# Sliding-window attention beside an MLP: output scaled while turned, rows of two heads dealt into spare rows, and a fixed order of instructions

## The chip, the core and the metric

The kernel runs on one core of a Trainium2 chip. The metric is the device time in microseconds, the median of three runs. A core has a matrix engine (TensorE, PE in the profile, with its weight loads as PEld), VectorE (DVE), ScalarE (ACT), GpSimd (POOL), SyncE (SP), which here only issues transfers, and 16 DMA engines. Matrix products go to PSUM, eight banks of 128 partitions by 512 f32; everything else lives in SBUF.

## The reference

One token sequence of 2048 with 448 features is normalized. Branch A is a local attention (16 heads of 28 features, each query sees eight keys at distances 0, 2, ..., 14) with an output projection. Branch B is an MLP of width 1792. The result is x + A * silu(B).

```python
x = A_x
xn = _layernorm(x, axis=-1)
# A: 16 heads of 28, window 8, dilation 2
qkv = (xn @ wqkv).reshape(B, S, 3, H, Dh)
idx = pos[:, None] - 2 * jnp.arange(8)[None, :]      # masked where < 0
logits = jnp.einsum("bhsd,bhswd->bhsw", q, kg) * Dh ** -0.5
o = jnp.einsum("bhsw,bhswd->bhsd", softmax(logits), vg)
s = o.reshape(B, S, D) @ wo
# B
h = gelu(xn @ w1 + b1)
g = silu(h @ w2 + b2)
return x + s * g
```

## The kernel before

**Tiles and stages.** Tokens are held with the even ones first and the odd ones behind, so that a window with dilation 2 becomes one of eight neighbours. There are 16 tiles of 128 tokens and four chunks of four tiles. For each tile, DVE takes statistics and normalizes (`stats`, `norm`), the normalized rows are turned (by TensorE for the first four tiles, by transposing DMAs on SP's queue for the others), and q, k and v are projected (L595, L618). q and k are turned by transposing DMAs; v goes out to memory and comes back in the layout of the windows. FF1 (L671) makes the hidden layer of a chunk in 14 blocks, with gelu on ACT (L675); FF2 (L703, L725) brings it back, and `gate` computes silu: on DVE the bias (L737), on ACT tanh or silu (L749, L744), on DVE the product (L753).

**Row halves.** 448 = 3 x 128 + 64. To use the array fully, most products run as 64-row passes, two tiles at a time: `pair` (L534) issues the passes of tile a on the upper 64 rows beside those of tile b on the lower 64, then the other way round, each tile into its own bank. Between the two halves the banks change their row half, so an empty instruction on POOL's queue (L551) waits for the first half, and the second half waits for it. TensorE does other passes in between. For q, k, v and FF1 a pair has 4 + 3 passes a tile, since the last 64 features stand on both halves of the rows; for FF2 it has 14 + 14.

**Attention.** Nine visits of 228 tokens each (224 in the middle). A visit has the scores (L770, four banks), exp on ACT (L779), masks on DVE (L785) and the values (L799), which leave two banks: bank a holds, on partitions 32g to 32g+27, a head's 28 output features, on partition 32g+28 the sum of the weights, in columns the tokens of two heads per group. `output_of` divides, per bank, by four instructions on DVE: a 32x32 transpose of the bank to `dt` (L808), the reciprocal of the sums (L812), a second transpose that spreads the reciprocals over the partitions (L817), and the product of bank and spread reciprocals into `oT` (L822). The bank is free only after the last of them.

**Output projection.** `oT` and `wo` have four kt of 128 rows; in each group of 32 rows, 28 are features and four are not (of wo they are zero, set by POOL at the start, L370). `final` (L853) makes the output projection. Tiles 0 to 13 go in pairs, with all four kt in either half:

```python
pair(job(t), job(t + 1), prio, False, (range(KT),), (range(KT),))
```

Tiles 14 and 15 have four passes of the full 128 rows each (L871), between which the last parts of their FF2 run. `gated` (L877) multiplies by the gate (L885, L883), adds x (L890) and sends the tile out on SP's queue (L894).

**Order.** Every instruction or group of them is a task of `_Plan`, with an engine, a cost, its dependencies, buffers that it takes and gives back, and a priority. `run` (L102) is a list scheduler: of the tasks of an engine that could start first, it takes the one with the highest priority (PRIO, LATER, NUDGE). The emitted program has one fixed order for each engine, so a wait of one instruction holds all behind it on that engine. At the start, tasks of TensorE that multiply constants (L346) fill its time until the plan's 8 us; those that would start later are left out.

Of the kernel before, what the change touches and what calls it, by code (L numbers as in the profile page):

```python
# [14 lines left out]
SLACK = 0.12  # L15
TABLE = 1.28
SWITCH = 0.095
TILED = 30
BURST = 3.5
NUDGE = {  # L20
    61: 4, 64: -20, 140: -165, 160: -221, 163: -244, 165: -29, 397: 111, 413: -37, 490: 163, 669: -149,
}
LAST = 352
SAME = 20
# [24 lines left out]
class _Task:  # L49
    __slots__ = ("eng", "cost", "deps", "fn", "prio", "take", "give", "slots",  # L50
# [3 lines left out]
class _Plan:  # L54
# [7 lines left out]
    def add(self, eng, cost, fn, deps=(), prio=0, take=(), give=(), tail=0.0, table=(), limit=None,  # L62
            mode=128):
# [4 lines left out]
        t.fn, t.prio, t.give, t.tail, t.table, t.limit = fn, prio, give, tail, table, limit  # L68
# [9 lines left out]
        t.prio += NUDGE.get(t.seq, 0)  # L78
# [6 lines left out]
    def _at(self, t, e, free):  # L85
        at = free.get(e, 0.0)
        for p, n in t.take.items():
            if len(p.free) < n or p.fifo and p.fifo[0] is not t:
                return None
            at = max(at, sorted(p.free)[n - 1][0] + HOP)  # L90
        if t.table and self.table not in t.table:
            at += TABLE
        for d in t.deps:
            at = max(at, d.end - d.tail if d.on == e else d.end + HOP)
        if e == "PE" and t.mode != self.mode:
            at = max(at, free.get(e, 0.0) + SWITCH)
        return at

    def _ready(self, t):
        return max([d.end - d.tail if d.on == "DMA" else d.end + HOP for d in t.deps], default=0.0)  # L100

    def run(self):  # L102
# [4 lines left out]
        free = {}  # L107
        self.table = None
        self.mode = 128
        ready = [t for t in self.tasks if not t.ndep]  # L110
        order = []
        while ready:
            cand = []
            for t in ready:
                ways = []
                for e, c in zip(t.eng, t.cost):
                    at = self._at(t, e, free)
                    if at is not None:
                        ways.append((at + (c if len(t.eng) > 1 else 0.0), at, e, c))
                if ways:  # L120
                    _, at, e, c = min(ways)
                    cand.append((at, t, e, c))
            if not cand:
                raise RuntimeError("the plan is stuck: " + str([(t.seq, t.eng, t.fn.__qualname__) for t in ready[:20]]))
            first = min(cand, key=lambda k: k[0])
            near = [k for k in cand if k[2] == first[2] and k[0] <= first[0] + SLACK]
            tiled = first[2] == "PE" and self.mode < 64
            at, t, e, c = min(near, key=lambda k: (self._ready(k[1]) if k[2] == "DMA" else -k[1].prio - (TILED if tiled and k[1].mode < 64 else SAME if k[2] == "PE" and k[1].mode == self.mode else 0),
                                                   k[0], k[1].seq))
            if t.limit is not None and at > t.limit:  # L130
                t.fn, c = None, 0.0
            t.on, t.start = e, at
            if e == "PE" and t.fn is not None:
                self.mode = t.out or t.mode
            if t.table and self.table not in t.table:
                self.table = t.table[0]
            free[e] = at + c
            t.end = at + c + t.tail
            for p, n in t.take.items():
                got = sorted(p.free)[:n]  # L140
                for g in got:
                    p.free.remove(g)
                t.slots[p] = [g[1] for g in got]
                t.after += [g[2] for g in got]
                if p.fifo is not None:
                    p.fifo.pop(0)
            for p, owner, i in t.give:
                p.free.append((t.end, owner.slots[p][i], t.seq))
            ready.remove(t)
            order.append(t)  # L150
            for u in t.users:
                u.ndep -= 1
                if not u.ndep:
                    ready.append(u)
        assert len(order) == len(self.tasks)
        self.order = sorted(order, key=lambda t: (t.start, t.seq))
        self.span = max(t.end for t in order)
        return self

# [19 lines left out]
def kernel(  # L179
# [62 lines left out]
    b1r = sb("b1r", [P, P])  # L242
# [6 lines left out]
    oT = sb("oT", [P, KT, S])  # L249
# [7 lines left out]
    zero = sb("zero", [P, H * 32])  # L257
# [4 lines left out]
    def ring(name, n, shape, dt=BF16, fifo=False):  # L262
# [5 lines left out]
    p_dt = ring("dt", 2, [P, 512], F32)  # L268
    p_rd = ring("rd", 2, [P, H], F32)
    p_y = ring("y", 2, [P, D], F32)  # L270
    p_t = ring("t", 2, [P, D], F32)
# [6 lines left out]
    p_h = ring("h", 28, [P, CH], fifo=True)  # L278
    p_v = ring("v", 3, [P, 4, H // 2, 32], fifo=True)
# [6 lines left out]

    PRIO = {
        "project": (54, 6.5, -1, -796,),
        "project2": (-47, -24.5, -697.5, -972,),
        "values": (-60, -238.5, -708, -812.5,),  # L290
        "attn": (332.5, 150, 124.5, 209.5, 61, 182.5, 339.5, 196.5, 276,),
        "ff1": (75, 107.5, 161, -24.5, -31, 92, 171.5, -1, -8, 117.5, 54, 79.5, 64, 6.5, 40, 96.5,
            13.5, 22.5, -0.5, 30, 190, 161.5, 181, 165.5, 181, 129, 104, 64.5,),
        "gelu": (-8, 79.5, 28, 194.5,),
        "ff2": (91.5, -34.5, -96.5, 114.5, 129.5, 89, -831.5, 135, 120, 180.5, 59, 104, 147.5, 131,
            -12.5, -48,),
        "final": (207.5, 2, 71.5, -16.5, 55.5, -2, 174.5, 203, 37, 65.5, -16, 162.5, 87.5, 134, 36,
            -5,),
        "norm": (131, 11, 219.5, 294, 62, 220, -31, 168.5, 7, 29.5, 162.5, 183.5, -110, 4.5, 164,
            134,),  # L300
        "loads": (227.5, 186, 183, 40, 129.5, 100, 27, -66,),
        "stats": (49, 32, 205.5, 205.5, 112, 82, 130.5, -5, 44.5, 27, 147.5, 207.5, 114, 203.5,
            217, 161,),
        "turn_x": (198, 4.5, 200, 12.5, 259, 121, 98.5, 186.5, 57, 57, 72, 135.5, 79, 58, 135, 88,),
        "turn_qk": (18.5, 126, 116, 140, -16, 32.5, 118.5, -91.5, 79.5, 15, 161.5, 121.5, 77.5,
            162.5, 166, -17.5,),
        "move_v": (129.5, 145.5, 200.5, 147.5, 126, 210.5, 218.5, 150, 100.5,),
        "store_v": (103, 80.5, 21.5, 52, 191, 92, 149, 31, 118, 150, 333.5, -0.5, 106, 223.5, 214,
            111,),
        "spread": (-10.5, 75.5, 298, 99.5, 52.5, 186.5, 149.5, -55, 104,),  # L310
        "copies": (187, 4, 219, 15.5, 90, 177, 88.5, 31, 29, 20.5, 182, 51, 204.5, 49.5, 24,),
    }
    LATER = {"swap": 191.5, "qk": 27, "v": 148, "gelu": 32.5, "exp": 149.5, "mask": -4394.5, "pv": -29.5, "recip": 100, "os": 224, "y": 202, "tanh": 79.5, "g": 204, "sg": 165.5, "o": 222.5}
# [28 lines left out]
    t_on = plan.add("DMA", 0.7, lambda _: None, (), 100)  # L342
    t_warm = t_on
    for i in range(48):
        def fn(k, n=512 if i < 9 else P):
            nc.tensor.matmul(buf(p_b, k)[:, :n], ones[:, :P], ones[:, :n], start=True, stop=True)  # L346
        t_warm = plan.add("PE", 0.427 if i < 9 else 0.107, fn, [t_warm], 1000 if i < 12 else -1000, take=(p_b,), limit=8.0)
        t_warm.give = ((p_b, t_warm, 0),)
    t_eps = plan.add("DVE", 0.07, memset("vector", eps_t[:], EPS), [t_on], prio=99)
    t_eps = plan.add("DVE", 0.07, memset("vector", half_t[:], -0.5), [t_eps], prio=99)  # L350
# [5 lines left out]
    t_ident = plan.add("POOL", 0.55, mk_ident, [t_on], prio=99)  # L356

    t_qz = [plan.add("DVE", 0.08, memset("vector", q[:, :, :, DH:], 0.0), [t_on], prio=95) for q in qk_tok]
    t_vw = [plan.add("DVE", 0.08, memset("vector", v[:, :, :, DH:], 1.0), [t_on], prio=96) for v in v_tok]
    t_kz = plan.add("DVE", 0.12, memset("vector", qkT[:, :, :, :PAD], 0.0), [t_on], prio=92)  # L360
# [330 lines left out]
    def ff2(t, prio):  # L691
        c, j = divmod(t, TPC)
        if t >= NT - 2:
            t_g[t] = []
            for cs, n, end in parts(t)[:1]:
                ff2_part(t, cs, n, end, prio - 0.1 * end)
# [359 lines left out]
```

## Time and profile before

| | us |
|---|---|
| runs | 152.48, 152.04, 152.18 |
| median | 152.18 |
| span of the profiled execution, first to last instruction | 150.4 |

The span leaves out what lies around it in a run, 1.78 us against the median; the time of the profiled execution as a whole is not given beside its span. In the profile, a line of a group reads: source line, engine, operation, output <- input, partitions x elements and type, count | busy us, mean ns of one | idle time of the engine just before it, and what ended it. Lines of the chain and of the timeline begin with start and length in us. DMA shares in the page are means over 16 engines.

### The profile page before, as it was taken

How to read it: one execution, taken by the hardware profiler on the slowest of the kernel's cores; microseconds unless marked ns; L12 is line 12 of the kernel's file. 1: busy time of each engine (PE TensorE's matmuls, PEld its weight loads, DVE VectorE, ACT ScalarE, POOL GpSimd, SP SyncE). 2: the span in 40 equal slices, each digit the busy share in tenths (PEclk: the TensorE clock that was granted, in tenths of full speed). 3: DMA queues.
4: the chain of work that ended last, by engine and by line, in shares of the span. 5: the costliest groups of instructions: out<-in, count | busy, mean ns of one | idle time of the engine just before them, and what ended most of it. 6: DMA issues, size and time to landing. Idle time of an engine off the chain costs nothing.

```text
span 150.4 us, 5216 instructions
## 1 busy us (share of the span) xinstructions
PE 146.1 (97%) x2173; PEld 76.9 (51%) x2173; DVE 113.7 (76%) x276; ACT 96.0 (64%) x168; POOL 18.4 (12%) x51
## 2 busy tenths in 40 slices
PE   7999999999999999999999999999999999999990
PEld 2644444544455555558556554445556445555460
DVE  3876850495546889899997989497998978995962
ACT  3365877658496594785788648888567497822020
POOL 7425530201750000011000000000000000000000
PEclk9999999999999999999999999999999999999999
DMA  4999869889999957159967994521120000001212
GB/s 155 327 314 362 126 124 159 261 119 361 185 161 197 72 100 139 37 114 226 125 201 175 147 256 128 125 74 38 36 65 7 0 0 4 4 0 61 63 63 63
DMA packets 38470, 19.47 MB, mean 129 GB/s; under 512 B 24887, under 2 KB 37758, under 8 KB 38446
## 3 DMA queue, kind: packets, MB, share of 16 engines
q1 hardware_dynamic: 37790, 17.84, 53.9%
q0 software_dynamic: 512, 1.18, 4.5%
q8 instruction: 17, 0.28, 0.8%
q10 hardware_dynamic: 144, 0.11, 0.2%
q14 instruction: 7, 0.06, 0.1%
HBM read 9.42 MB, written 3.94 MB: 89 GB/s over the span
## 4 chain that ended last, share of the span: by engine, by line
PE 97%; DVE 0%; ACT 0%; issue 0%
PE bank L671 28%; PE bank L703 25%; PE bank L595 14%; PE bank L618 7%; PE bank L863 7%; PE bank L799 4%; PE bank L725 4%; PE bank L346 3%; PE bank L770 3%; PE bank L871 1%; PE bank L519 1%; DVE sg L883 0%; ACT w_in L744 0%; PE bank L503 0%; DVE o L890 0%; PE bank L723 0%
## 5 line engine op out<-in xcount | busy, mean ns | idle before, releaser
L671 PE MATMUL bank<-xnT,w 64*128 64x512 bf16 x392 | 44.1, 376 | 0.0
L675 ACT ACTIVATE h<-bank,b 128x512 bf16<-128x512 f32 x56 | 34.5, 687 | 11.7 <-PE bank L671 11.5
L703 PE MATMUL bank<-w,h 64*128 64x448 bf16 x392 | 40.2, 349 | 0.0
L671 PEld LDWEIGHTS <-w 64*128 64x128 bf16 x392 | 18.8, 94 | 22.1
L703 PEld LDWEIGHTS <-h 64*128 64x128 bf16 x392 | 18.6, 94 | 16.8
L595 PE MATMUL bank<-w_in,xnT 64*128 64x448 bf16 (+1 forms) x212 | 24.8, 350 | 0.0
L779 ACT ACTIVATE E<-bank 128x456 bf16<-128x456 f32 (+1 forms) x36 | 16.9, 554 | 9.9 <-PE bank L770 8.6
L331 ACT CAST qk_tok<-bank 128x448 bf16<-128x448 f32 x25 | 12.3, 539 | 5.9 <-PE bank L595 4.8
L595 PEld LDWEIGHTS <-xnT 64*128 64x128 bf16 (+1 forms) x212 | 10.8, 94 | 9.4 <-DVE xnT L333 0.2
L808 DVE STREAM_TRANSPOSE dt<-bank 128x480 f32<-128x480 f32 (+1 forms) x18 | 12.1, 673 | 4.5 <-PE bank L799 4.5
L618 PE MATMUL bank<-w_in,xnT 64*128 64x448 bf16 (+1 forms) x106 | 14.0, 350 | 0.0
L863 PE MATMUL bank<-wo,oT 64*128 64x448 bf16 x112 | 12.6, 349 | 0.0
L817 DVE STREAM_TRANSPOSE dt<-rd 128x480 f32<-128x480 f32 (+1 forms) x18 | 12.1, 675 | 0.6
L822 DVE TENSOR_TENSOR oT<-bank,dt 128x456 bf16<-128x456 f32 (+1 forms) x18 | 11.4, 632 | 0.6
L785 DVE TENSOR_TENSOR E<-E,m_gen 128x456 bf16<-128x456 bf16 (+1 forms) x32 | 10.8, 390 | 0.0
L443 DVE BATCH_NORM_STATS2 st<-x_sb 128x6 f32<-128x448 bf16 x16 | 9.5, 606 | 1.7 <-DMA x_sb<-in_A_x_dram 1.7
L333 DVE CAST qk_tok<-bank 128x448 bf16<-128x448 f32 x7 | 4.3, 620 | 8.6 <-PE bank L595 8.6
L737 DVE TENSOR_TENSOR y<-bank,b 128x448 f32<-128x448 f32 x15 | 8.7, 619 | 1.9 <-PE bank L703 1.8
L749 ACT ACTIVATE t<-y 128x448 f32<-128x448 f32 x12 | 6.7, 583 | 4.0 <-DVE y L737 4.0
L484 DVE TENSOR_SCALAR xn<-x_sb,mv,rstd 128x448 bf16<-128x448 bf16 x16 | 6.3, 393 | 3.6 <-POOL rstd L466 3.4
L744 ACT ACTIVATE w_in<-y 128x448 bf16<-128x448 f32 x3 | 1.7, 577 | 10.9 <-DVE y L737 10.9
L863 PEld LDWEIGHTS <-oT 64*128 64x128 bf16 x112 | 5.8, 94 | 4.8 <-issue 0.2
(76 smaller groups left out, 143.5 us busy)
## 6 DMA issues: line engine op xcount, KB each, us to landing
v<-v_hbm SPq DMA_DIRECT2D x16, 128.0 KB, 3.2
out_dram<-o SPq DMA_DIRECT2D x15, 112.0 KB, 2.0
v_hbm<-v_tok SPq DMA_DIRECT2D x13, 128.0 KB, 3.5
w<-in_B_w_dram SPq DMA_DIRECT2D x2, 672.0 KB, 6.7
w_in<-in_A_wqkv_dram SPq DMA_DIRECT2D x3, 336.0 KB, 4.2
x_sb<-in_A_x_dram SPq DMA_DIRECT2D x4, 224.0 KB, 4.1
w<-in_B_w_dram SPq DMA_DIRECT2D x2, 448.0 KB, 7.8
w<-in_B_w_dram SPq DMA_DIRECT2D x2, 336.0 KB, 8.9
```

Source lines behind the costliest of these rows:

```text
L331: nc.scalar.copy(o, i)
L595: return nc.tensor.matmul(ps[:, :D], xnT[r, kt, cs], w, start=start, stop=stop)
L618: return nc.tensor.matmul(ps[:, :D], xnT[r, kt, k0:k0 + P], w, start=start, stop=stop)
L671: return nc.tensor.matmul(ps[:], w1[r, kt, ms], xnT[r, kt, cs], start=start, stop=stop)
L675: nc.scalar.activation(buf(p_h, own, i)[:], buf(p_b, own, i)[:], ACT.Gelu_apprx_tanh, bias=b1[:, mt:mt + 1])
L703: return nc.tensor.matmul(ps[:, :D], buf(*h_at[(c, mt)])[r, cs], w2[r, mt, :], start=start, stop=stop)
L779: nc.scalar.activation(buf(p_E, k)[:, :8 * n], buf(p_b, a, at + i)[:, :8 * n], ACT.Exp, scale=SCALE)
L785: nc.vector.tensor_tensor(out=E, in0=E, in1=m[:, :, :, :n].rearrange("p i g q -> p (i g) q"), op=ALU.mult)
L808: nc.vector.transpose(buf(p_dt, k)[:, :32 * m], buf(p_b, po, i)[:, :32 * m])
L817: nc.vector.transpose(buf(p_dt, d)[:, :32 * m].rearrange("p (b c) -> p b c", c=32), buf(p_rd, r)[:, :m].unsqueeze(2).to_broadcast((P, m, 32)))
L822: nc.vector.tensor_tensor(out=oT[:, a::2, q:q + 4 * n1], in0=buf(p_b, po, i)[:, :n].rearrange("p (l q) -> p l q", l=2), in1=buf(p_dt, d)[: ...
L863: return nc.tensor.matmul(ps[:, :D], oT[r, kt, t * P:(t + 1) * P], wo[r, kt, :], start=start, stop=stop)
```

## The change

It has three parts.

1. **Attention output.** Per bank: a transpose of all 512 columns to an f32 tile (the bank is free after it), the reciprocal, the product in the turned layout (tokens on partitions, 28 features of a head together), written as bf16 over the same tile, and a bf16 transpose into `oT`. Before this last transpose four small copies per visit, on POOL or ACT, put the rows of the two heads that bank 1's second half holds on partitions 0 to 63 into the four spare columns of every group of 32. So kt 0, 1 and 2 have 128 feature rows each and kt 3 has 64, on its lower half.
2. **Output projection.** wo is loaded in the same arrangement (eight loads instead of four, no zeroing), and its 64 rows of kt 3 are copied to the upper half. `final` runs three kt in the first half of a pair and four in the second. For odd tiles up to 13 the lower rows of kt 3 of `oT` are copied to the upper ones; for tiles 14 and 15 the upper rows are set to zero.
3. **Order.** The scheduler and its priorities go; a list ORDER names the tasks by number, in the order in which they are placed; a negative number takes the second engine of a task that has two. Buffers change too: `dt`, `y` and `t` share one ring of six, `b1r` and `zero` use buffers of other rings. Three output tiles (8, 9, 10) leave in two transfers each.

```diff
-NUDGE = {
...
+ORDER = [
+    53, 49, 50, 126, 1, 82, 64, 54, 56, 52, 2, 3, 4, 5, 83, 6, 7, 8, 9, 10, 11, 86, 87, 88, 66, 90, 68, 70, 72, 74,
...
+]
+TWICE = (8, 9, 10)
...
-        while ready:
...
+        for n in ORDER:
+            self._place(self.tasks[max(n, ~n)], int(n < 0))
...
-    oT = sb("oT", [P, KT, S])
+    oT = sb("oT", [P, KT, S + 32])
...
-    p_dt = ring("dt", 2, [P, 512], F32)
+    b1r = p_E.bufs[1][:, :P]
+    p_dt = p_y = p_t = ring("wide", 6, [P, 512], F32)
...
-    t_wo = [plan.add("POOL", 1.6, memset("gpsimd", wo[:], 0.0), [t_ident], prio=98)]
...
-                            c0, c1 = (4 * h + s) * n, (G * (s % 2) + g) * n
+                            c0, c1 = 256 * h + s * n, (G * (s % 2) + g) * n
...
+    def turned_in(d):
+        return buf(p_dt, d)[:].bitcast(BF16)[:, :512].rearrange("p (l b c) -> p l b c", l=2, c=32)
+
+    def output_of(b, po):
         q, n1 = VIS[b]
+        d, m = [], []
+        for a in range(2):
+            def f5(k, a=a):
+                nc.vector.transpose(buf(p_dt, k)[:], buf(p_b, po, a)[:])
+            d.append(plan.add("DVE", dve(512), f5, [po], take=(p_dt,), give=((p_b, po, a),)))
+        for a in (1, 0):
+            def f6(k, a=a):
+                nc.vector.reciprocal(buf(p_rd, k)[:], buf(p_dt, d[a])[:].rearrange("p (b c) -> p b c", c=32)[:, :, DH])
+            r = plan.add("DVE", 0.25, f6, [d[a]], take=(p_rd,))
+
+            def f7(k, a=a, r=r):
+                nc.vector.tensor_tensor(out=turned_in(d[a]).rearrange("p l b c -> p (l b) c")[:, :, :DH],
+                                        in0=buf(p_dt, d[a])[:].rearrange("p (b c) -> p b c", c=32)[:, :, :DH],
+                                        in1=buf(p_rd, r)[:].unsqueeze(2).to_broadcast((P, H, DH)), op=ALU.mult)
+            m.insert(0, plan.add("DVE", dve(D), f7, [r], give=((p_rd, r, 0),)))
+        for a in range(2):
+            moved = []
+            for x in range(2):
+                def f8(k, a=a, x=x):
+                    i = turned_in(d[1])[:64, 1, :, :DH].rearrange("p b (g c) -> p g b c", c=4)[:, 3 * x + a:3 * x + a + 3:2]
+                    o = turned_in(d[a])[64 * x:64 * x + 64, :, :, DH:]
+                    if k.on == "ACT":
+                        nc.scalar.copy(o, i)
+                    else:
+                        nc.gpsimd.tensor_copy(o, i)
+                moved.append(plan.add(("POOL", "ACT"), (0.3, 0.21), f8, [m[0], m[1]]))
+
+            def f9(_, a=a):
+                nc.vector.transpose(oT[:, a::2, q:q + 256], turned_in(d[a]).rearrange("p l b c -> p l (b c)"))
+            o = plan.add("DVE", dve(512), f9, moved + turned_out[a][-1:], give=((p_dt, d[a], 0),))
...
+                    t_up[t] = [plan.add(("POOL", "ACT"), (0.35, 0.26), f, t_oT[t])]
+                elif t >= NT - 2:
+                    t_up[t] = [plan.add("POOL", 0.25, memset("gpsimd", oT[:64, 3, t * P:(t + 1) * P], 0.0), t_oT[t])]
...
-            pair(job(t), job(t + 1), prio, False, (range(KT),), (range(KT),))
+            pair(job(t), job(t + 1), False, (range(3),), (range(KT),))
...
+        pieces = 2 if t in TWICE else 1
+        w, left = n // pieces, []
...
-    t_wo += [dma("POOL", wo[32 * g:32 * g + 28, :, :], A_wo[112 * g:112 * g + 112, :].rearrange("(l c) d -> c l d", l=4),
-                 100, 80, [t_w2[1][0]] + t_wo[:1]) for g in range(G)]
+    t_wo = []
+    for g in range(G):
+        k, at = 3 + g // 2, (112 * (g % 2) + 84) + 12 * (g // 2)
+        t_wo.append(dma("POOL", wo[32 * g:32 * g + 28, :k, :], A_wo[112 * g:112 * g + 28 * k, :].rearrange("(l c) d -> c l d", l=k), 25 * k, [t_w2[1][0]]))
+        t_wo.append(dma("POOL", wo[32 * g + 28:32 * g + 32, :k, :], A_wo[at:at + 4 * k, :].rearrange("(l c) d -> c l d", l=k), 4 * k, [t_w2[1][0]]))
+    t_wo.append(plan.add("POOL", 0.9, lambda _: nc.gpsimd.tensor_copy(wo[:64, 3, :], wo[64:, 3, :]), t_wo[4:]))
```

Of ORDER, the stretches that the prediction follows, counted out into instructions, read on TensorE: from visit 2's values pass to the first output projection, FF2 of tiles 2/3 (second half, first part), first halves of q/k/v of tiles 12 to 15 with their second halves, the rest of that FF2, more of the same projections, and then the output projection of tiles 0/1; between the last visit's values pass and tile 14's projection, the end of FF1, the projections of tiles 10/11, FF2 of 12/13, the projection of 12/13 around tile 14's FF2.

More of the change, by code (lines that the diff above doesn't have):

```diff
@@ L83, in add @@
         return t
[L85 to L100, printed above, removed]
     def run(self):
@@ L106, in run @@
                 d.users.append(t)
[L107 to L111, printed above, removed]
-        while ready:
[L113 to L154, printed above, removed]
@@ L155, in run @@
[L155 to L158 removed]
+        self.free, self.table, self.mode, self.order = {}, None, 128, []
+        for t in self.tasks:
+            if not t.ndep and t.eng[0] in AT_ONCE:
+                self._place(t, 0)
+        for n in ORDER:
+            self._place(self.tasks[max(n, ~n)], int(n < 0))
+        assert len(self.order) == len(self.tasks)
```

373 lines of the change are left out of this document (181 added, 192 removed), and 41 rows, old and new, of the table ORDER.

## The prediction

> **What bounds the kernel now.** I read the page first: the busy shares and the chain that ended last.
>
> ```profile
> span 150.4 us, 5216 instructions
> PE 146.1 (97%) x2173; PEld 76.9 (51%) x2173; DVE 113.7 (76%) x276; ACT 96.0 (64%) x168; POOL 18.4 (12%) x51
> PEclk9999999999999999999999999999999999999999
> PE 97%; DVE 0%; ACT 0%; issue 0%
> ```
>
> 97% of the chain lies on TensorE, at the full granted clock throughout. A busy PE can still hide waits, since its ends are modelled, so I went on to the chain in order of time (start, length, what) and compared the same kind of pass at different places.
>
> ```profile
> 0.83 4.75 PE bank L346 x16
> 5.58 0.32 PE bank L519 x2
> 5.90 0.11 PE bank L346
> ...
> 60.49 0.57 PE bank L618 x6
> 66.52 0.76 PE bank L618 x8
> ...
> 83.95 0.57 PE bank L618 x6
> 84.52 1.32 PE bank L703 x14
> ...
> 92.62 4.53 PE bank L671 x42
> ...
> 114.12 0.63 PE bank L799 x39
> 114.75 0.54 PE bank L770 x32
> ...
> 136.79 3.03 PE bank L863 x32
> 139.82 2.75 PE bank L725 x14
> ...
> 146.21 0.61 PE bank L725 x14
> ...
> 147.41 0.21 DVE o L890
> ```
>
> A 64-row pass of 448 columns costs 0.0946 us wherever it stands: 0.757/8, 1.32/14, 3.03/32 = 0.0947. One of 512 columns costs 4.53/42 = 0.108. So a pair's half of eight passes is 0.76 us, of six 0.57, of fourteen (FF2) 1.32; an FF1 half is 0.86 or 0.65. The lines that have many passes agree as wholes:
>
> ```profile
> L671 PE MATMUL bank<-xnT,w 64*128 64x512 bf16 x392 | 44.1, 376 | 0.0
> L703 PE MATMUL bank<-w,h 64*128 64x448 bf16 x392 | 40.2, 349 | 0.0
> L863 PE MATMUL bank<-wo,oT 64*128 64x448 bf16 x112 | 12.6, 349 | 0.0
> ```
>
> (Busy time counts the overlap of neighbours; passes times spacing gives 42.4, 37.1 and 10.6 us.) From 5.58 us to 146.8 us TensorE is a wall: what is added to its passes is paid in full, and what another engine gains is worth nothing unless the wall has a hole. After it comes a tail of some 3.6 us (last gate, product, sum, transfer), before it 5.6 us of loads and first statistics.
>
> **The change part by part.** The sum is made against the span, 150.4 us; the three runs have a median of 152.18, so 1.78 us lie around the span, and I carry them along unchanged.
>
> *Seven passes instead of eight.* The seven paired output projections (tiles 0 to 13) issue 112 passes at L863. After: three kt in the first half, four in the second, for two tiles and two halves of rows each, 6 + 8 = 14 instead of 16 per pair, 98 in all. Both halves stay side by side on the array (each first-half pass of one tile runs next to a second-half pass of the other), so no pass is left alone. Fourteen fewer at 0.0946 us: **-1.32 us**, on the wall. The two last tiles keep four full passes each (L871), as their top rows are zeroed instead: 0.
>
> *The attention output.* Per bank, before and after, on DVE:
>
> ```profile
> L808 DVE STREAM_TRANSPOSE dt<-bank 128x480 f32<-128x480 f32 x16 | 10.8, 676 | 2.8 <-PE bank L799 2.8
> L808 DVE STREAM_TRANSPOSE dt<-bank 128x448 f32<-128x448 f32 x2 | 1.3, 645 | 1.6 <-PE bank L799 1.6
> L812 DVE RECIPROCAL rd<-dt 128x15 f32<-128x15 f32 x16 | 4.0, 251 | 0.5
> L817 DVE STREAM_TRANSPOSE dt<-rd 128x480 f32<-128x480 f32 x16 | 10.9, 678 | 0.6
> L822 DVE TENSOR_TENSOR oT<-bank,dt 128x456 bf16<-128x456 f32 x16 | 10.1, 633 | 0.6
> L753 DVE SCALAR_TENSOR_TENSOR g<-t,y 128x448 bf16<-128x448 f32 x10 | 5.8, 615 | 0.0
> L785 DVE TENSOR_TENSOR E<-E,m_gen 128x456 bf16<-128x456 bf16 x30 | 10.1, 390 | 0.0
> ```
>
> Before: 676 + 251 + 678 + 633 = 2.24 us. After: a transpose of 512 elements (676 and 645 give 0.97 ns an element, so about 707), a reciprocal of 16 (about 252), a product of 448 from two f32 tiles in SBUF (nearest: 615), and a bf16 transpose of 512. No row has a bf16 transpose; its bounds are the bf16 product at 390 and the f32 transpose at 707, and I take the upper end, the row of its own operation: 2.28 us. Eighteen banks: +0.8 us of DVE, with the lower end -5. The page "VectorE: DVE Perf Modes" of the Trainium skill, section "The three transpose paths", gives 311 ns for a bf16 block of 128 columns; with the fixed part of the two f32 rows, about 200 ns, that is again near 1 ns an element, and the upper end. On the path this costs nothing as long as DVE keeps up: it was busy 113.7 of 150.4 us. The PSUM banks come free after the first transposes rather than after the product, about 1.5 us earlier each; with no hole in the wall I count that at 0.
>
> *Dealt rows.* Four copies of 64x64 per visit, 36 in all; by the new list 13 stand on ACT and 23 on POOL; seven copies of 64x128 (one on ACT), two zeroings on POOL, and one copy of half of wo. The nearest rows:
>
> ```profile
> L492 POOL COPY xn<-xn 128x64 bf16<-128x64 bf16 x4 | 0.9, 236 | 4.7 <-DVE xn L484 4.7
> L466 POOL TENSOR_TENSOR rstd<-sd,half_t 128x4 f32<-128x4 f32 x2 | 2.1, 1036 | 0.2
> L331 ACT COPY xnT<-bank 128x256 bf16<-128x256 bf16 x3 | 1.1, 373 | 2.3 <-PE bank L519 2.3
> ```
>
> On POOL 0.24 to 1.04 us each (the new ones move runs of four elements; the upper row is the slowest arithmetic that POOL has); I take 0.3, the copy's row with some more. On ACT at most 0.37. Work added to POOL: 23 x 0.3 and about 3 us for the rest, some 10 us on an engine that has 18; to ACT 5 us beside 96. Both are covered by the wall. But POOL also carries the empty instruction between the halves of every pair (L551), which TensorE's second half waits for, so a late copy delays it. I followed the new list: behind six of the groups of copies there is such an instruction, with 0.9 to 3.1 us of passes as cover. At 0.3 a copy nothing shows: **0**.
>
> *The longest new chain.* The list puts the first output projection behind the deal of visits 0 and 1 and the copy of tile 1's rows. From the end of visit 2's values pass, TensorE has six halves of eight (0.76), five of six (0.57) and two of fourteen (1.32) before it: 4.5 + 2.8 + 2.6 = 10.0 us (rounded). DVE has in that time five 32x32 transposes out, two in, two reciprocals, two products, two sums, two masks, one cast, from the rows above 9.3 us by durations (sums and cast as the 615 row). Neighbours that do not depend on each other start some 0.08 us before the last one ends:
>
> ```profile
> 134.26 0.62 DVE L885 SCALAR_TENSOR_TENSOR sg<-bank,g 128x448 bf16<-128x448 f32 x1
> 134.92 0.39 DVE L890 TENSOR_TENSOR o<-x_sb,sg 128x448 bf16<-128x448 bf16 x1
> 135.23 0.62 DVE L885 SCALAR_TENSOR_TENSOR sg<-bank,g 128x448 bf16<-128x448 f32 x1
> ```
>
> which leaves 8.4 us, then one copy on POOL and two hand-overs, 0.6: 9.0 of 10.0. It fits with a microsecond to spare. At the end, the last two tiles have 11 us of passes between visit 8 and their use, and DVE about 9 us of work.
>
> *The order.* The greedy planner gives way to a fixed list. Passes are the same but for the 14; fillers at the start (L346) are 17 up to the end of tile 0's transposes, as before, and then as many of seven as fall before the plan's 8 us: 0 to 7 at 0.11 us. Before, one came; I take two, **+0.1 us**. The load order at the start is the same. wo comes in eight loads instead of four, on POOL's queue at
>
> ```profile
> L374 POOL DMA_DIRECT2D wo<-in_A_wo_dram x4 | 2.5, 620 | 0.0
> L338 POOL MEMSET wo<- 128x1792 bf16 x1 | 1.6, 1581 | 0.0
> ```
>
> 0.62 each, +2.5 us spread over several pairs; the zeroing of wo, 1.6, goes. The first use of wo is over 30 us later. Three output tiles leave in two transfers, three more issues on SP, which idles then: 0.
>
> Sum: 150.4 - 1.32 + 0.1 = 149.2 us of span, **151.0 us** in the runs' measure.
>
> **Rivals.**
>
> *A: the deal is late at some visits.* A product on DVE has now two inputs in SBUF where before one came from PSUM, and POOL copies run beside it. Nothing in this trace shows how the two get on: POOL is idle from 70 us on, by its line of forty slices of 3.76 us:
>
> ```profile
> POOL 7425530201750000011000000000000000000000
> ```
>
> If each of a visit's four copies waits for half a product (0.31), the chain above is 1.2 us longer and uses up its margin, and TensorE waits 0.2 there; with three products at 0.62 in its way as well, half of that each, 1.1 in all. I take 0.8: **151.8 us**. Against it: the other visits have 1.7 us and more. The Trainium skill, page "SBUF — State Buffer", section "Who interferes with whom", speaks for it: a DVE instruction with two SBUF inputs and a GpSimd one that reads SBUF exclude each other, the later one waiting for the whole of the earlier. By that rule this rival is real for some of the 23 copies; no run here shows it yet.
>
> *B: the wall also shrinks elsewhere.* All passes at their spacing (90.1 us for the three lines above, the rest from the other lines) make up about 140.3 of the 141.2 us between 5.58 and 146.8, fillers left out; 0.9 us are switches and small waits. Earlier banks and a list without priorities could take half: **150.5 us**. For it: DVE's queue was full exactly where banks were needed (9.3 of 10 us in the next fence, whose columns are the stretch, its length and the busy time of PE, PEld, DVE, ACT and POOL). Against: the chain has 0% of issue, so no wait worth naming.
>
> ```profile
> 60.00:70.00 10.00, 10.00 (x175) 6.20 (x173) 9.29 (x20) 7.31 (x14) 1.14 (x2) 1.00 0.46 110
> 70.00:80.00 10.00, 10.00 (x219) 5.79 (x215) 9.36 (x20) 7.54 (x15) 0.00 (x0) 1.00 0.92 174
> 110.00:120.00 10.00, 10.00 (x218) 5.57 (x216) 9.28 (x22) 6.05 (x12) 0.00 (x0) 1.00 0.06 16
> ```
>
> *C: slower, by POOL's queue.* If a copy of four-element runs costs nearer the 1.04 row, the groups of three or four copies in front of the empty instruction outlast their cover. At 0.8 us each: before the pair of tiles 12/13's projections (four copies, a load, the copy of wo: 4.8 against 3.9 of cover, +0.9), before two FF1 pairs of the last stage (1.6 against 0.9, +0.7 each) and before the FF2 of tiles 10/11 (+0.1): 2.4 us lost, **153.4 us**; at 1.04 the same places lose 5.4. It decides from some 0.65 us a copy, where they lose what the passes gain. Against: the copy row at 236 ns.
>
> *D: the new head eats the gain.* All seven fillers run, five more than I count (0.55), and the pairs that the list moves ahead of the first FF1 wait for the turned x of tile 3 as long as its two copies take (373 ns each by the row of ACT, 0.75): **152.3 us**. Against: the chain showed no such wait before, with the same loads.
>
> **How the numbers follow.** Forecast 0.50, A 0.13, B 0.15, C 0.14, D 0.08. About 0.3% (0.46 us) is what a measurement of this kernel can tell from no change. Faster by more: the forecast, B, and half of A, 0.72; within: the other half of A and most of D and a little of C, 0.14; slower: the rest of C and D, 0.14. The range takes in B with a free bank or two more and the milder end of C: 150.0 to 152.8.
>
> **What would show it.** Right: 98 passes of the projection's 64-row form at 0.0946 us spacing, the chain still 97% PE, 17 to 24 fillers, span about 149.2. The bf16 transpose's row near 700 ns and POOL's small copy near 300. Wrong: a wait of PE on POOL before a second half (C), PE waiting for oT at the first projection at some 78 us (A), DVE products or POOL copies in long and short forms of one shape (A), PE idle before the first FF1 (D). The forecast fails if the wall has a hole of over 1 us anywhere.

## The result and the profile after

| us | before | after |
|---|---|---|
| runs | 152.48, 152.04, 152.18 (shown); 152.22 median of the six beside after | 150.79, 150.25, 150.25, 151.02, 150.21, 151.15 |
| median | 152.22 | 150.52 |
| ratio, 95% interval | | 0.9882 (0.9853 to 0.9911) |
| span of the profiled execution | 150.4 | 149.1 (of 150.79 us) |

The changed kernel is faster by 1.7 us, 1.2%; 151.0 was forecast, with 149.2 for the span. The page of the changed kernel, in its lines of totals and the shares of the chain:

```profile
span 149.1 us, 5240 instructions
PE 144.4 (97%) x2158; PEld 74.5 (50%) x2158; DVE 107.0 (72%) x271; ACT 102.9 (69%) x187; POOL 27.8 (19%) x84
PE 94%; DMA 2%; DVE 2%; issue 0%; ACT 0%
```

TensorE is busy 1.7 us less, VectorE 6.7 us less, ScalarE 7 us more, GpSimd 9 us more, and the chain is as before TensorE's, but for the head, which the chain now follows to the first load of x. Its pieces (start, length, what) at the head and around the first output projection:

```profile
0.80 2.58 DMA x_sb<-in_A_x_dram
3.40 0.64 DVE st L424
...
79.84 0.57 PE bank L867 x6
80.41 0.57 PE bank L575 x6
80.98 0.76 PE bank L867 x8
```

The first half of a pair has now six passes in 0.57 us, the second eight in 0.76: still 0.095 us each, and nothing stands between the pieces, so the first projection did not wait for the deal. The groups of the changed steps (columns as explained with the profile of before):

```profile
L867 PE MATMUL bank<-wo,oT 64*128 64x448 bf16 x98 | 11.6, 349 | 0.0
L791 DVE STREAM_TRANSPOSE wide<-bank 128x512 f32<-128x512 f32 x18 | 12.3, 702 | 5.1 <-PE bank L779 5.1
L795 DVE RECIPROCAL rd<-wide 128x16 f32<-128x16 f32 x18 | 4.2, 241 | 0.2
L799 DVE TENSOR_TENSOR wide<-wide,rd 128x448 bf16<-128x448 f32 x18 | 11.2, 626 | 0.4
L816 DVE STREAM_TRANSPOSE oT<-wide 128x512 bf16<-128x512 bf16 x18 | 12.2, 694 | 0.7 <-POOL wide L812 0.5
L812 POOL COPY wide<-wide 64x64 bf16<-64x64 bf16 x23 | 6.6, 305 | 47.4 <-PE bank L651 19.3 <-DVE wide L799 15.0 <-ACT wide L810 5.8
L810 ACT COPY wide<-wide 64x64 bf16<-64x64 bf16 x13 | 2.9, 241 | 2.3 <-DVE wide L799 2.3
```

Per bank 702 + 241 + 626 + 694 = 2.26 us on VectorE. The bf16 transpose (694) has the price of the f32 one, and the copy on GpSimd has the mean that was assumed (what that mean is made of stands under rival A below). VectorE waited 0.5 us in all for a copy (the idle time of L816).

### The profile page after: what moved, and what is told of

It reads as the page before. It is cut to its first block, busy times and chain, and to the rows that moved or that the text cites. A ratio compares the mean times of both kernels' runs of the same rounds, so it can differ in the third digit from the quotient of the medians.

```text
span 149.1 us, 5240 instructions
## 1 busy us (share of the span) xinstructions
PE 144.4 (97%) x2158; PEld 74.5 (50%) x2158; DVE 107.0 (72%) x271; ACT 102.9 (69%) x187; POOL 27.8 (19%) x84
## 4 chain that ended last, share of the span: by engine, by line
PE 94%; DMA 2%; DVE 2%; issue 0%; ACT 0%
PE bank L651 29%; PE bank L683 25%; PE bank L575 15%; PE bank L598 7%; PE bank L867 6%; PE bank L779 4%; PE bank L705 4%; PE bank L750 3%; DMA x_sb<-in_A_x_dram 2%; PE bank L875 1%; DVE st L424 1%; PE bank L499 1%; DVE xn L464 0%; DVE sg L887 0%; ACT w_in L724 0%
## 5 line engine op out<-in xcount | busy, mean ns | idle before, releaser
L651 PE MATMUL bank<-xnT,w 64*128 64x512 bf16 x392 | 44.8, 376 | 0.0
L651 PEld LDWEIGHTS <-w 64*128 64x128 bf16 x392 | 18.7, 94 | 22.2
L313 ACT CAST qk_tok<-bank 128x448 bf16<-128x448 f32 x27 | 13.4, 536 | 7.1 <-PE bank L575 5.0
L791 DVE STREAM_TRANSPOSE wide<-bank 128x512 f32<-128x512 f32 x18 | 12.3, 702 | 5.1 <-PE bank L779 5.1
L812 POOL COPY wide<-wide 64x64 bf16<-64x64 bf16 x23 | 6.6, 305 | 47.4 <-PE bank L651 19.3
L816 DVE STREAM_TRANSPOSE oT<-wide 128x512 bf16<-128x512 bf16 x18 | 12.2, 694 | 0.7 <-POOL wide L812 0.5
L717 DVE TENSOR_TENSOR wide<-bank,b 128x448 f32<-128x448 f32 x15 | 8.9, 615 | 3.9 <-PE bank L683 2.2
L867 PE MATMUL bank<-wo,oT 64*128 64x448 bf16 x98 | 11.6, 349 | 0.0
L799 DVE TENSOR_TENSOR wide<-wide,rd 128x448 bf16<-128x448 f32 x18 | 11.2, 626 | 0.4
L635 ACT ACTIVATE kd<-qkT,head 128x1024 bf16<-128x1024 bf16 x10 | 11.2, 1157 | 0.0
L313 ACT CAST v_tok<-bank 128x448 bf16<-128x448 f32 x13 | 6.6, 537 | 4.6 <-issue 3.9
L729 ACT ACTIVATE wide<-wide 128x448 f32<-128x448 f32 x12 | 7.0, 579 | 3.2 <-DVE wide L717 3.1
```

Source lines behind the costliest of these rows:

```text
L313: nc.scalar.copy(o, i)
L635: nc.scalar.activation(dst, src, ACT.Copy, scale=head[:, a:a + 1])
L651: return nc.tensor.matmul(ps[:], w1[r, kt, ms], xnT[r, kt, cs], start=start, stop=stop)
L791: nc.vector.transpose(buf(p_dt, k)[:], buf(p_b, po, a)[:])
L816: nc.vector.transpose(oT[:, a::2, q:q + 256], turned_in(d[a]).rearrange("p l b c -> p l (b c)"))
L867: return nc.tensor.matmul(ps[:, :D], oT[r, kt, t * P:(t + 1) * P], wo[r, kt, :], start=start, stop=stop)
```

## The experiments

**How they are read.** A run's time has three parts: a head of loads, the stretch in which TensorE never waits, and the end. Heads and ends turned out to differ by some tenths from build to build and from execution to execution, as much as most effects here. So beside each time I compare the middle stretch in the profile: from the start of the first FF1 pass (L651, in before L671) to the start of the last sum (`o`, L894, in before L890). Both are the first and last start of one line; the line numbers shift by one to three in edited kernels, and the last digit is 0.1 us. Kernels with different orders have their first FF1 at different places of the list, so the stretch is compared within the family of before and within that of after.

**The changed kernel again**

> The changed kernel as it is, the measure for the other runs of this group. Both theories: 150.5 us within 0.5. Its six executions so far lay at 150.2 and at 151.0, so a profile near 148.5 us of span, where the one at hand has 149.1, would show at which place the 0.6 us differ: I expect at the head, before the first transposes, since the rest of TensorE's row is the same list of instructions; the rival is that they are spread over waits in the middle.

Measured: 150.54 us (150.13 to 150.82, before beside it 152.44). The view of one line for each end of the stretch (minimum, median and maximum of its durations in ns, then first and last start), first of the profile after, then of this one:

```profile
L651 PE MATMUL bank<-xnT,w x392: 376/376/387, 14.7 to 130.2; 64*128 64x512 bf16 x196
L894 DVE TENSOR_TENSOR o<-x_sb,sg x17: 207/384/420, 83.0 to 146.4; 128x448 bf16<-128x448 bf16 x15, 128x352 bf16<-128x352 bf16 x1, 128x96 bf16<-128x96 bf16 x1
```

```profile
L651 PE MATMUL bank<-xnT,w x392: 375/376/388, 14.7 to 130.1; 64*128 64x512 bf16 x196
L894 DVE TENSOR_TENSOR o<-x_sb,sg x17: 207/385/418, 82.9 to 146.2; 128x448 bf16<-128x448 bf16 x15, 128x352 bf16<-128x352 bf16 x1, 128x96 bf16<-128x96 bf16 x1
```

The stretch has 131.7 and 131.5 us. Six profiles have this list of TensorE and lose nothing in the middle, these two and four below: in five of them the first FF1 starts between 14.4 and 14.8 us with 131.5 to 131.7 behind it, in the sixth at 15.1 with 131.6. So the middle repeats to 0.2 us and the head spreads over 0.7. The two profiles of the changed kernel itself came too close to each other, 0.3 us of span, to show what sets its executions at 150.2 and at 151.0 apart.

**Eight passes again, in the changed kernel**

```diff
-            pair(job(t), job(t + 1), False, (range(3),), (range(KT),))
+            pair(job(t), job(t + 1), False, ((0, 1, 2, 0),), (range(KT),))
```

> The changed kernel with eight 64-row passes again in the output projection (the pass of the first 128 input rows is issued twice in the first half of each pair of tiles, so the output is not the reference's). My theory, that TensorE's row sets the time and the eighth pass is paid in full: 14 x 0.0946 = +1.32 us over the changed kernel, so 151.8, and the slow part of the 1.7 us gained is here. Rival, that the passes went behind waits of TensorE that the new order removed: under +0.4 us, 150.9 or less.

Measured: 151.78 us, +1.24 over the changed kernel beside it. The view of the two lines in this kernel:

```profile
L651 PE MATMUL bank<-xnT,w x392: 375/376/388, 14.6 to 130.9; 64*128 64x512 bf16 x196
L894 DVE TENSOR_TENSOR o<-x_sb,sg x17: 208/385/417, 83.0 to 147.4; 128x448 bf16<-128x448 bf16 x15, 128x352 bf16<-128x352 bf16 x1, 128x96 bf16<-128x96 bf16 x1
```

The stretch is 132.8, 1.2 more. The passes are paid in full, as the theory says; the rival's 0.4 is out.

**Before, a second profile, and before with seven passes**

> The kernel before as it is, for a second profile of it. Its first profile was of an execution of 152.04 us, at the low end of the executions of before (median 152.44 in the last group). If the head varies in it as in the changed kernel, this profile differs from the first before TensorE's first projection of scores, by up to 0.4 us, and is the same list of distances behind it. Rival: that it differs at the end, behind the last matmul, where the stores go out.

```diff
-            pair(job(t), job(t + 1), prio, False, (range(KT),), (range(KT),))
+            pair(job(t), job(t + 1), prio, False, ((0, 1, 2),), (range(KT),))
```

> The kernel before with its own order and its own way of scaling the attention output, but with seven 64-row passes in place of eight in the output projection of the first 14 tiles (the last pass of the first half is left out, so the output is not the reference's). My theory, that the passes alone carry most of the gain: 14 x 0.0946 = 1.32 us less, or 1.24 as the run with eight passes in the changed kernel measured it, so 151.15 within 0.2, and 0.6 us of the gain are left for the order and the ends. Rival, that before has waits into which the gain of the passes falls: above 151.7.

Measured: 151.96 us for the one execution of before, and 150.84 with seven passes against 152.14 beside it: -1.30, ratio 0.9914 (0.9887 to 0.9941). The two lines, in before and then with seven passes:

```profile
L671 PE MATMUL bank<-xnT,w x392: 376/376/388, 12.9 to 129.4; 64*128 64x512 bf16 x196
L890 DVE TENSOR_TENSOR o<-x_sb,sg x17: 208/392/393, 70.4 to 147.2; 128x448 bf16<-128x448 bf16 x15, 128x352 bf16<-128x352 bf16 x1, 128x96 bf16<-128x96 bf16 x1
```

```profile
L671 PE MATMUL bank<-xnT,w x392: 376/376/387, 13.2 to 128.7; 64*128 64x512 bf16 x196
L890 DVE TENSOR_TENSOR o<-x_sb,sg x17: 209/393/393, 70.5 to 145.9; 128x448 bf16<-128x448 bf16 x15, 128x352 bf16<-128x352 bf16 x1, 128x96 bf16<-128x96 bf16 x1
```

From 134.3 to 132.7: 1.6 by these rounded starts, 1.5 by unrounded ones. In this family the middle repeats less well than in the other: by unrounded starts it has 134.1, 134.2 and 134.1 us in three profiles with eight passes (the first of before, this one, and the one with split stores below), and 132.7 and 133.1 in the two with seven, so 1.2 less by the means. In time it is 1.3; the greedy order of before, left as it was, gains by the passes at once. What the change brings beyond is 1.7 - 1.3 = 0.4 us.

**Without the copies, and the longer product alone.** Three kernels: no copies at all, no copies on GpSimd, all copies; each with the longer product.

```diff
-in0=buf(p_dt, d[a])[:].rearrange("p (b c) -> p b c", c=32)[:, :, :DH],
+in0=buf(p_dt, d[a])[:].rearrange("p (b c) -> p b c", c=32),
...
-                        nc.gpsimd.tensor_copy(o, i)
```

> The changed kernel without its 36 copies of 64x64 blocks (13 on ACT, 23 on POOL); the spare columns get their own scaled values from a product that is 64 columns longer, so the output is not the reference's. My theory, that the copies are hidden: 0.0 us against the changed kernel, within 0.2. Rival A of the forecast, that the copies come late or collide with VectorE's products and hold the projection: 0.3 to 0.8 us faster.

> The changed kernel without the 23 copies on POOL; those 13 on ACT stay, since without them the load of a function table came to stand behind a wait for TensorE. The product is 64 columns longer, as in the run before (the output is not the reference's). My theory, copies hidden: 150.5, within 0.2 of the changed kernel. Rival A, copies that hold the chain or VectorE: 0.3 to 0.8 us less.

> The changed kernel with nothing but the longer product (128x512 in place of 128x448, about 70 ns more for each of 18), all 36 copies as they are: the control for the two runs without copies. My theory: 0.0, within 0.2 of 150.5, since VectorE has the room. Rival, that the longer product itself is what cost 1.4 us in the run without copies: 151.5 or more.

Measured: 151.94, 151.45 and 150.40 us. The longer product costs nothing (150.40 against 150.54 of the changed kernel in the group before). Its row, and the ends of its middle, 131.6 us:

```profile
L799 DVE TENSOR_TENSOR wide<-wide,rd 128x512 bf16<-128x512 f32 x18 | 12.4, 694 | 0.4
```

```profile
L651 PE MATMUL bank<-xnT,w x392: 376/376/388, 14.4 to 129.9; 64*128 64x512 bf16 x196
L894 DVE TENSOR_TENSOR o<-x_sb,sg x17: 207/384/420, 82.7 to 146.0; 128x448 bf16<-128x448 bf16 x15, 128x352 bf16<-128x352 bf16 x1, 128x96 bf16<-128x96 bf16 x1
```

And without copies the kernel is *slower*, by 1.4 and 1.0, which neither theory had. The profiles tell why it is not the copies. First no copies on GpSimd (an execution of 151.85 us, 0.4 above the median of this kernel):

```profile
L651 PE MATMUL bank<-xnT,w x392: 376/376/387, 15.1 to 130.5; 64*128 64x512 bf16 x196
L892 DVE TENSOR_TENSOR o<-x_sb,sg x17: 208/384/393, 83.3 to 146.7; 128x448 bf16<-128x448 bf16 x15, 128x352 bf16<-128x352 bf16 x1, 128x96 bf16<-128x96 bf16 x1
```

The stretch is 131.6, like that of the kernel with all copies: the theory holds, and rival A is out for the copies on GpSimd. The rest is the head and the end, 0.7 us each against the kernel with the longer product. In the head the same loads land later. The timeline of this kernel, and below it the same instruction of the kernel with the longer product alone:

```profile
8.60 0.35 PE L575 MATMUL bank<-w_in,xnT 128*128 128x448 bf16 x1 [0.21 <-DMA w_in<-in_A_wqkv_dram]
9.04 0.63 DVE L424 BATCH_NORM_STATS2 st<-x_sb 128x6 f32<-128x448 bf16 x1 [0.75 <-DMA x_sb<-in_A_x_dram]
```

```profile
8.44 0.63 DVE L424 BATCH_NORM_STATS2 st<-x_sb 128x6 f32<-128x448 bf16 x1 [0.29 <-DMA x_sb<-in_A_x_dram]
```

That is 0.6 us. At the end the last store took 2.1 us from issue to landing where the changed kernel's took 1.5. The view of the transfers around the issue of that store shows another one there, a fetch of instructions on queue q14. In this kernel it falls among the packets of the last stores, in the changed kernel ahead of them. The rows (packets, MB, share of 16 engines; then the store), no copies on GpSimd from 146.9 to 148 us, the second profile of the changed kernel from 145.9 to 147:

```profile
q14 instruction: 1, 0.01, 3.8%
...
out_dram<-o SPq DMA_DIRECT2D x1, 24.0 KB, 2.1
```

```profile
q14 instruction: 1, 0.01, 2.6%
...
out_dram<-o SPq DMA_DIRECT2D x1, 24.0 KB, 1.5
```

That the fetch delays the store, and that the shorter list of GpSimd moved it, fits the times but was not tried by itself.

The kernel without any copies loses 0.6 us in the middle as well. Its ScalarE loads the function table for exp behind a wait for the scores, where the changed kernel loads it ahead of them (timelines of ScalarE, the second profile of the changed kernel first), and the first output projection behind that stands still, 0.6 us when its starts are matched with those of the changed kernel:

```profile
103.53 1.28 ACT L759 ACT_TABLE_LOAD   x1
```

```profile
104.96 1.28 ACT L759 ACT_TABLE_LOAD   x1 [1.21 <-PE bank L750]
...
106.86 0.72 PE L864 MATMUL bank<-wo,oT 64*128 64x448 bf16 x5 [0.24 <-ACT E L759]
```

Taking copies away rearranged the waits of the instructions around them, and one of these waits came to stand ahead of the load. This run therefore says nothing about the price of the 13 copies on ScalarE.

**Two and three times the copies on GpSimd**

```diff
-                        nc.gpsimd.tensor_copy(o, i)
+                        for _ in range(3):
+                            nc.gpsimd.tensor_copy(o, i)
```

> The changed kernel with each of the 23 copies on POOL made three times, so about 0.8 to 0.9 us for each in place of 0.305. The forecast's case of POOL's queue (the empty instruction between the two halves of a pair stands behind the copies) has its turning point at 0.65 us for a copy and 153.4 us at 0.8: by it 2 to 3 us slower than the changed kernel. Rival, that the copies have far more room than I gave them: under +0.3 us.

> The changed kernel with each of the 23 copies on POOL made twice: about 0.55 to 0.6 us for each. With three times the copies TensorE stood still at two places for POOL's empty instruction, 0.40 and 0.55 us. If the forecast's turning point of 0.65 us holds, nothing is lost here: 150.5 within 0.15. Rival, that the margin is already used up by the single copies: half of the loss seen with three, 0.35 us more.

Measured: 151.29 with three, +0.75, between the 2 to 3 us of the theory and the 0.3 of its rival; 151.11 with two, +0.6 over the 150.5 of the earlier groups. With three, the timeline has two places where TensorE waits for GpSimd's empty instruction (L531 here, L551 in before), behind the copies of the rows above:

```profile
71.43 0.80 POOL L813 COPY wide<-wide 64x64 bf16<-64x64 bf16 x2
...
72.42 0.74 PE L575 MATMUL bank<-w_in,xnT 64*128 64x448 bf16 x6 [0.24 <-POOLq L531]
...
118.29 1.83 POOL L813 COPY wide<-wide 64x64 bf16<-64x64 bf16 x6 [6.80 <-PE bank L651]
...
119.94 0.82 PE L651 MATMUL bank<-xnT,w 64*128 64x512 bf16 x6 [0.38 <-POOLq L531]
```

Matched start by start with the changed kernel, TensorE loses 0.40 us at the first and 0.55 at the second; elsewhere behind the head it loses nothing (it gains 0.1 at 53.9 us, as the second profile of the changed kernel does). That is the mechanism of rival C, at two of the four places that it named, 0.95 us where it had 2.4. At the first place C had counted the load and the copy of wo in front of the empty instruction; in the trace that instruction runs at 72.35 us, ahead of the copy of wo at 72.90. With two copies, the two lines:

```profile
L651 PE MATMUL bank<-xnT,w x392: 376/376/387, 14.8 to 130.3; 64*128 64x512 bf16 x196
L895 DVE TENSOR_TENSOR o<-x_sb,sg x17: 209/385/423, 83.0 to 146.4; 128x448 bf16<-128x448 bf16 x15, 128x352 bf16<-128x352 bf16 x1, 128x96 bf16<-128x96 bf16 x1
```

131.6: not a tenth is lost in the middle at twice the copies, so the margin is not used up. In time the run came out as its rival said, but not by TensorE waiting for the copies: of the 0.5 us of span between this profile and the second one of the changed kernel, 0.2 lie in the head and 0.3 behind the last landing. There the instruction with which GpSimd clears the semaphores starts at 148.84 us, 0.30 us behind the start of TensorE's last one, where in the second profile of the changed kernel it starts 0.01 behind; what held it stayed open.

**The place of the last stores.** The second profile of before had pointed to the end: from the start of the last sum to the end of the span it has 150.2 - 147.2 = 3.0 us, the changed kernel 148.8 - 146.2 = 2.6. There SP goes through a row of ten waits in a fixed order, the last eight of which are for the eight semaphores that SP's own transfers signal in turn (SP's queues, in what follows). Counted from the wait that ends when the last store but one has landed, SP's list of such instructions shows, in the second profiles of before and of the changed kernel:

```profile
L1051 SPq EVENT_SEMAPHORE  x7: 28/28/28, 148.8 to 149.3; - x7
```

```profile
L1063 SPq EVENT_SEMAPHORE  x2: 28/28/28, 147.6 to 147.9; - x2
```

In before five waits with nothing left to wait for come behind the last landing, 0.06 us each; in the changed kernel none. The changed kernel issues five transfers more on SP: three stores that are split, and two stores of v (15 on SP where before had 13), which before POOL's queue issued. So I gave before five stores more, by sending tiles 4 to 8 in halves, alone and together with the seven passes, and sent the three split stores of the changed kernel whole again.

```diff
-            (nc.scalar if k.on == "ACT" else nc.sync).dma_start(rows(o_half, t * P, P)[:, cs], buf(p_o, o)[:, :n])
+            for c in range(0, n, n // 2 if 4 <= t < 9 else n):
+                w = n // 2 if 4 <= t < 9 else n
+                (nc.scalar if k.on == "ACT" else nc.sync).dma_start(rows(o_half, t * P, P)[:, cs.start + c:cs.start + c + w], buf(p_o, o)[:, c:c + w])
```

> The kernel before, with the stores of tiles 4 to 8 issued in two halves each: five more stores, which move the last two stores from the queues that SP waits for early in its row of ten waits at the end to the last two of that row. Theory: the waits behind the last landing go from five to none, 5 x 0.06 = 0.3 us less than before, so about 151.9 where before has 152.2; the span behind the last sum on VectorE shrinks from 2.8 to 2.5. Rival: that this end is noise of the store's own time, or that five more issues cost as much: no difference, within 0.1.

> The kernel before with both: seven passes (one left out, so the output is not the reference's) and the five stores in halves. Theory, that the passes and the place of the last stores are the whole gain of the change: 1.30 + 0.3 = 1.6 us less than before, about 150.5 to 150.6, the time of the changed kernel within 0.15. Rival, that the new order or the earlier release of the banks holds a share of its own: 150.85, as with the seven passes alone, or over 0.2 us above the changed kernel.

> The changed kernel with its three split stores whole again: three stores fewer, so that the last two lie three waits earlier in SP's row. Theory: 3 x 0.06 = 0.2 us slower than the changed kernel (150.4 to 150.5), about 150.65. Rival: no difference, or faster by the three issues saved.

Measured: before with five more stores 152.01 against 152.27, -0.26, ratio 0.9982 (0.9961 to 1.0004), so in time alone just short of certain. The same waits in it, and in the changed kernel with whole stores:

```profile
L1053 SPq EVENT_SEMAPHORE  x2: 28/28/28, 149.2 to 149.4; - x2
```

```profile
L1065 SPq EVENT_SEMAPHORE  x5: 28/28/28, 147.3 to 147.7; - x5
```

Five waits fewer than in before, and three more than in the changed kernel, as expected. From the last sum to the end of the span, before with five more stores has 150.3 - 147.6 = 2.7 (2.6 by unrounded starts), and the changed kernel with whole stores 148.7 - 145.9 = 2.8. In time the latter showed nothing, 150.54 where 150.65 was expected: the 0.2 us is too little for its four runs to tell, and its profiled head was early (first FF1 at 14.4).

Before with both edits, seven passes and five more stores: 150.59 us, ratio 0.9891 (0.9859 to 0.9923), where the changed kernel has 150.52, 150.54 and, with the longer product, 150.40. With its own order, and its own way of scaling, the kernel before comes within 0.2 us of the changed one.

## Why the prediction was right, and where it was off

- **Seven passes, -1.32.** Right: +1.24 when the eighth was put back, -1.30 when it was left out of before.
- **The attention output, 0.** Right: 2.26 us per bank where 2.28 was taken, the bf16 transpose at 694 ns where 707 was; and another 1.2 us of VectorE (18 products at 694 instead of 626) moved nothing in the run with the longer product. For VectorE as a whole the 0.8 us more did not come: it is busy 6.7 us less. Its durations add up to 3.6 us less, since the list gives three of the head products (`kd`) and three casts to ScalarE, which the forecast did not count, and its instructions overlap more. Off the wall this is worth nothing.
- **Dealt rows, 0.** Right: 305 ns on GpSimd where 300 was taken, 241 on ScalarE where at most 373 was. That the 305 met the 300 is luck: it is the mean of 13 copies of some 230 ns and ten that rival A's effect made longer. The middle has 131.6 us with the 23 copies of GpSimd, without them, and with twice as many. For ScalarE's 13 it is only argued, since the run without them was disturbed by the table.
- **The longest chain, 9.0 of 10.0 us.** It fitted; no piece of the chain waits at 79.84.
- **Rival A.** Its mechanism is there, its loss isn't. One shape of copy comes short and long (minimum, median, maximum of the line), and a long one starts beside a product with two inputs in SBUF (the line, then timelines of GpSimd and VectorE):

```profile
L812 POOL COPY wide<-wide x23: 227/233/514, 68.9 to 129.6; 64x64 bf16<-64x64 bf16 x23
```

```profile
98.61 0.48 POOL L812 COPY wide<-wide 64x64 bf16<-64x64 bf16 x1 [0.40 <-DVE o L894]
```

```profile
98.38 0.61 DVE L733 SCALAR_TENSOR_TENSOR g<-wide,wide 128x448 bf16<-128x448 f32 x1
```

  The product ends at 98.99 us, the copy at 99.09. It is so throughout this trace: ten of the 23 copies take 264 to 514 ns, and each of them runs beside a VectorE instruction with two inputs in SBUF and ends 91 to 96 ns behind the end of it. The other 13 take 227 to 237, among them those beside transposes, those beside products with an input in PSUM, and one that met only the last 0.13 us of a product. So a copy lost 0.03 to 0.28 us where A took 0.31 for each, 13 lost nothing, and the cover of the wall hid the rest. The Trainium skill, page "SBUF — State Buffer", section "Who interferes with whom", has the later of the two wait for the whole of the earlier; the trace agrees, by those 91 to 96 ns.
- **Rival C.** The place was right and the price too high: at 0.8 us a copy 0.95 us are lost instead of 2.4, and at the single copies' 0.3 nothing.
- **Rival D.** It did not come: 17 fillers ran, and between the first transpose of x and the first FF1 TensorE stands idle for 0.06 us in all in the first profile and not at all in the second.
- **The order, +0.1.** It was 0 or a little less: 17 fillers ran instead of the 19 that I took. The order and the earlier release of the banks, taken together with the rest, leave no more than 0.2 us between the changed kernel and before with both edits. The 150.5 us of rival B is what was measured, but by luck: its reason, a wall that shrinks elsewhere, did not show. From the first transpose of x (L519, in the changed kernel L499) to the start of the last pass (L871, L875) TensorE takes 141.3 to 141.7 us in the four profiles with eight passes, three in before's order and one in the new one, and 139.9 to 140.4 in six with seven, two in before's order and four in the new one. Neither order is ahead by more than it varies itself.
- **The step that was off.** "Three output tiles leave in two transfers, three more issues on SP, which idles then: 0", and with it the end of the span, which I carried along unchanged. As a cost it was 0; but the five issues more moved the last stores to the end of SP's row of waits, which gives back 0.3 us (3.0 to 2.6 or 2.7 in three profiles that have it, five waits at 0.06). With it and without the +0.1, the sum is 150.4 - 1.32 - 0.3 = 148.8 us of span. The second profile of the changed kernel has just that, the first 149.1; that one of them agrees to the digit is luck, since heads vary by more.

So of 1.7 us, the passes made 1.3 and the place of the last stores 0.3; what is left, 0.1, is below the spread of the head.

## What to carry to other kernels

Where one engine is a wall from head to end, count its instructions, price them by their spacing, and expect the rest of a rework, however large, at nothing. Then look at both ends, which an unchanged sum hides: which waits still run after the last store has landed, and on which queue that store lies. And where an experiment takes instructions away, compare the stretch in question and not the time alone, since heads, ends and the place of waits move with the build.

## What was not expected of the hardware

- At the end SP's waits for finished queues cost 0.06 us each even when they have nothing to wait for, so the number of transfers issued ahead, which decides on which queues the last ones lie, was worth 0.3 us here.
- The same first loads landed 0.6 us later in one build than in another (statistics of a tile of x at 9.04 and 8.44 us, first FF1 at 15.1 and 14.4). Not every shift of the head follows this tile: in the two profiles of the changed kernel its statistics start at 8.68 and 8.33 us and the first FF1 at 14.7 in both.
- A table load of 1.28 us was ahead of a wait in one build and behind it in another (103.53 and 104.96), from an edit that removed copies elsewhere on ScalarE and on GpSimd.
- A copy on GpSimd takes some 230 ns, but one that starts beside a VectorE instruction with two inputs in SBUF ended 0.09 us behind the end of that instruction, after up to 514 ns. The other way round, the one product of L799 that started during a copy took 708 ns, where the other 17 took 611 to 627.
